# Sparse attention followed by a bilinear FFN: even and odd rows of a half dealt to two matmul positions, padded activation sums, one store per half, and one-bank PSUM tiles in the last tile's second pass

## The chip, the cores and the metric

The kernel runs on one core of a Trainium2 chip. Times are device microseconds (us) of that core for one whole launch. The core has five instruction queues that run beside each other[...]: TensorE (PE, with its weight loads shown apart as PEld), VectorE (DVE), ScalarE (ACT), GpSimd (POOL) and SyncE (SP, which only issues transfers). A line number such as L650 is a line of the kernel before the change, unless it is said to be of the changed kernel.

## The reference

Two stages are computed, the second on the output of the first. The shapes are batch 8, heads 8, sequence 576, head width 64; so 4608 tokens of width 512 enter the FFN, whose inner width is 1536.

```python
scores = scale * np.matmul(q, k.transpose(0, 1, 3, 2))
mask_local = (rel >= 0) & (rel < stride)                          # heads 0 to 3, stride 32
mask_strided = (rel >= 0) & (pos[None, :] % stride == pos[:, None] % stride)   # heads 4 to 7
...
attn = np.exp(scores - max); attn = attn / (sum + 1e-09)
x = (attn @ v).transpose(0, 2, 1, 3).reshape(4608, 512)
out = ((x @ w_a) * (x @ w_b)) @ w_out
```

## The kernel before

The work is cut twice. Attention goes batch by batch (b from 0 to 7) and each batch into eight units (S: scores, exponential and mask; V: product with v and division). The FFN goes by nine tiles of 512 tokens (t from 0 to 8). Tile t is 16 slots: slots 0 to 11 (`ffn_ab`, L548) make the inner activations of one block of 128 inner columns each. Two groups of matmuls of L545 give x·w_a and x·w_b in PSUM, ACT copies the first (L562), and DVE multiplies the two into the bf16 tile `pf` (L565). Slots 12 to 15 multiply `pf` by w_out. While the FFN of tile t runs, the attention of a later batch is put in between its matmuls, at places that the tables STEPS and LATER (L513 to L519) give, so that PE does not stand still for ACT and DVE. Tiles 7 and 8 have no attention left beside them.

Tiles 3 to 8 (FAST_Y) do the last product by a seven-product scheme for two by two blocks (Winograd's form of Strassen's scheme) in place of eight products. The tokens of a tile are split in two halves i, the output columns in two halves j, the inner dimension in even and odd blocks e. L565 writes `pf` so that the half i takes 256 columns in a row. DVE then forms five sums or differences of the quarters of `pf` (`fast_s`, L572 to L583) in the tile `ps`, numbered n = 0 to 4: L578 makes sum 0, L580 sums 1 and 2, L582 differences 3 and 4. They are made in parts, for ranges of the six pairs of inner blocks g, at the places that L868 gives: slot 4 (sum 0, g 0-1), 6 (3 and 4, g 0-1), 8 (1 and 2, g 0-1), 10 (3 and 4, g 2-3), 11 (sum 0, g 2-5; then 3 and 4, g 4-5), and 12 (1 and 2, g 2-5).

`y_plan` (L610) then runs the products in the order 3, 4, 1, 7, 5, 2, 6. Each is two positions q of six matmuls g (L650): 128 rows from `pf` or `ps` as the stationary operand, 256 columns from w_out or from a sum of its blocks as the moving operand. Products 3 and 4 read `pf`; product 1 reads sum 0, product 7 difference 4, product 5 sum 1, product 2 sum 2 and product 6 difference 3. Their results are put together by DVE (L626, L629, L631, L639), ACT (L622, L633, L635) and POOL (L636, L640), and `store_half` (L615) sends each half of the rows out on SP's queue by two transfers, one for each q.

The order of the instructions on every engine is the order in which the code issues them (`manual_schedule`, L742). Semaphore waits are put in by the framework, which compares the parts of a tile that two instructions read or write. [...]

The last tile, t = 8, uses `y_tail` (L656): first all seven products for position q = 0 (the first pass), then for q = 1 (the second pass), so that the first pass's rows leave early. The second pass has four accumulators, a, b, c and d. Before the change, a and b are the two banks of one PSUM tile (`o`), c and d the two banks of another (`st`). The order of the products is 3 (a), 4 (b), 1 (c), 2 (b), 5 (a), 6 (c), 7 (d); 3 and 4 are read by L683 and L685, 1 by L689, 2 by L693, 5 by L698, 6 by L703 and 7 by L706.

Of the kernel before, what the change touches and what calls it, by code (L numbers as in the profile page):

```python
# [7 lines left out]
F32 = mybir.dt.float32  # L8
BF16 = mybir.dt.bfloat16
I16 = mybir.dt.int16  # L10
ALU = mybir.AluOpType
# [19 lines left out]
def kernel(  # L31
# [10 lines left out]
    nc = tc.nc  # L42
# [7 lines left out]
    FD = d_ff // 128  # L50
    TTOK = 512
# [6 lines left out]
    nat = ctx.enter_context(tc.tile_pool(name="nat", bufs=1))  # L58
    sb = ctx.enter_context(tc.tile_pool(name="sb", bufs=3))
    fsb = ctx.enter_context(tc.tile_pool(name="ffn", bufs=2))  # L60
    pst = ctx.enter_context(tc.tile_pool(name="pst", bufs=1, space=bass.MemoryType.PSUM))
    dram = ctx.enter_context(tc.tile_pool(name="dram", bufs=2, space=bass.MemoryType.DRAM))

    psum4 = {}
# [98 lines left out]

    FG = FD // 2
    HT = TTOK // 2
    HN = d_model // 2
    wf = wp.tile([128, 5, FG, HN], BF16, name="wf")
    wov = wo_sb.rearrange("p (g e) (j n) -> p e j g n", e=2, j=2)
# [14 lines left out]
    shared = {}  # L183

    def load_qk(b, strided, heads=range(HL), names="kq"):
        for nm in names:
            src = {"k": k, "q": q}[nm]
            if b < FIRST_D:
                n, R, h0 = (NP, RS, HL) if strided else (96, RL, 0)
                w0 = {"k6": 0, "q6": 1536, "k8": 3072, "q8": 5120}[f"{nm}{R}"]  # L190
                if b not in shared:
                    shared[b] = nat.tile([128, 5 * FD * TTOK // 4], BF16, tag="shared", name="shared")
                t = nats[b, nm, strided] = shared[b][:n, w0:w0 + HL * R * D].rearrange("p (h r d) -> p h r d", r=R, d=D)
                hs = slice(heads[0], heads[-1] + 1)
                nc.gpsimd.dma_start(out=t[:, hs], in_=src[b, h0:h0 + HL].rearrange("h (p r) d -> p h r d", r=R)[:, hs])  # L195
            elif strided:

                t = nat_s[nm]
                n = 32 if b == FIRST_D else YS
                for h in heads:  # L200
                    nc.gpsimd.dma_start(
                        out=t[32 * h:32 * h + n],
                        in_=bass.AP(tensor=src.tensor, offset=(b * H + HL + h) * S * D,
                                    ap=[[RS * D, n], [YS * RS * D, 3], [1, RS * D]]))
            else:
                if 0 in heads:
                    nats[b, nm, strided] = nat.tile([128, NY, D], BF16, tag=f"{nm}l", name=f"{nm}l")
                t = nats[b, nm, strided]
                for h in heads:
                    nc.gpsimd.dma_start(out=t[32 * h:32 * h + 32],  # L210
                                        in_=src[b, h].rearrange("(i y) d -> y i d", y=32))
            nats[b, nm, strided] = t
# [127 lines left out]
    ps = {}  # L340
# [190 lines left out]
    def mm_bank(shape):  # L531
        nm = "tp" if used[0] % 4 == 3 and used[0] >= 0 else "mm"
        used[0] += 1
        return psum4[nm].tile(shape, F32, tag=nm, name="mm")
# [35 lines left out]
    pss = {}  # L570

    def fast_s(t, n, gs):  # L572
        if t not in pss:
            pss[t] = nat.tile([128, 5 * FD * TTOK // 4], BF16, tag="shared", name="ps").rearrange("p (g m) -> p g m", g=FG)
        s = pss[t][:, gs]
        x = pfs[t].rearrange("p (g e) (i m) -> p g e i m", e=2, i=2)[:, gs]
        if n == 0:
            nc.vector.tensor_tensor(s[:, :, 0:HT], x[:, :, 0, 0], x[:, :, 1, 1], op=ALU.add)  # L578
        elif n == 1:
            nc.vector.tensor_tensor(s[:, :, HT:3 * HT].rearrange("p g (i m) -> p g i m", i=2), x[:, :, 0], x[:, :, 1], op=ALU.add)  # L580
        else:
            nc.vector.tensor_tensor(s[:, :, 3 * HT:].rearrange("p g (e m) -> p g e m", e=2), x[:, :, :, 1], x[:, :, :, 0],  # L582
                                    op=ALU.subtract)  # L583

    yst = {}

    def products(t):
        pf, s = pfs[t], pss[t]
        full = lambda e, i: (lambda g, q: pf[:, 2 * g + e, HT * i + 128 * q:HT * i + 128 * (q + 1)])
        summed = lambda n: (lambda g, q: s[:, g, HT * n + 128 * q:HT * n + 128 * (q + 1)])  # L590
        wsum = lambda n: (lambda g: wf[:, n, g])
        wfull = lambda e, j: (lambda g: wov[:, e, j, g])
        return {"3": ("a", full(0, 0), wsum(0)), "4": ("b", full(1, 1), wsum(1)), "1": ("c", summed(0), wsum(2)),
                "2": ("b", summed(2), wfull(0, 0)), "5": ("a", summed(1), wfull(1, 1)), "6": ("c", summed(3), wsum(3)),
                "7": ("d", summed(4), wsum(4))}

    def f32t(nm):
        return fsb.tile([128, 2, HN], F32, tag=nm, name=nm, bufs=1)

    def col(j):  # L600
        return slice(HN * j, HN * (j + 1))

    def y_store(eng, t, y, i, q, n=slice(0, d_model)):
        rows = out[TTOK * t:TTOK * (t + 1), n].rearrange("(q a i s) c -> a s i q c", q=2, i=2, s=16)
        eng.dma_start(out=rows[:, :, i, q], in_=y[i][:, q, n])

    def y_bufs():
        return [fsb.tile([128, 2, d_model], F32, tag="y_sb", name="y_sb", bufs=2) for _ in range(2)]

    def y_plan(t):  # L610

        plan, bank, v = products(t), {}, {}
        y = []

        def store_half(i):  # L615
            for q in range(2):
                y_store(nc.sync, t, y, i, q)

        def post(k):
            if k == "3":  # L620
                v["a"] = v["w"] = f32t("ya")
                nc.scalar.copy(v["a"], bank["a"])  # L622
                y.extend(y_bufs())
                v["y"] = y
            elif k == "4":
                nc.vector.tensor_tensor(v["w"], bank["b"], v["a"], op=ALU.add)  # L626
            elif k == "1":
                v["e"] = f32t("ye")
                nc.vector.tensor_tensor(v["e"], bank["c"], v["w"], op=ALU.add)  # L629
            elif k == "7":  # L630
                nc.vector.tensor_tensor(v["e"], v["e"], bank["d"], op=ALU.subtract)  # L631
            elif k == "2":
                nc.scalar.copy(y[1][:, :, col(0)], bank["b"])  # L633
            elif k == "5":
                nc.scalar.copy(y[0][:, :, col(1)], bank["a"])  # L635
                do(16 * t + 15, nc.gpsimd.tensor_tensor, y[0][:, :, col(0)], v["e"], y[0][:, :, col(1)], ALU.subtract)  # L636
                do(16 * t + 18, store_half, 0)
            else:
                nc.vector.tensor_tensor(v["w"], bank["c"], v["w"], op=ALU.add)  # L639
                do(16 * t + 17, nc.gpsimd.tensor_tensor, y[1][:, :, col(1)], v["w"], y[1][:, :, col(0)], ALU.subtract)  # L640
                do(16 * t + 19, store_half, 1)

        for k in "3417526":
            b, lhs, rhs = plan[k]
            new = b not in bank
            if new:
                bank[b] = mm_bank([128, 2, HN])
            for q in range(2):
                for g in range(FG):
                    nc.tensor.matmul(bank[b][:, q], lhsT=lhs(g, q), rhs=rhs(g), start=new and q == 0 and g == 0,  # L650
                                     stop=g == FG - 1, skip_group_check=True)
                    if g == FG - 1 and q == 1:
                        post(k)
                    yield v

    def y_tail(t):  # L656

        plan, y = products(t), y_bufs()
        w, e = f32t("ya"), f32t("ye")
        v = {"a": w, "y": y}  # L660
        for q in range(2):
            if q == 0:
                bank = {x: mm_bank([128, HN]) for x in "abcd"}
            else:
                o = psum4["o"].tile([128, 2, 512], F32, tag="o", name="end")
                st = pst.tile([128, 2, 512], F32, tag="st", name="end")
                bank = {"a": o[:, 0, :HN], "b": o[:, 1, :HN], "c": st[:, 0, :HN], "d": st[:, 1, :HN]}
            c21, c12, c22 = y[1][:, q, col(0)], y[0][:, q, col(1)], y[1][:, q, col(1)]
            wq, eq = w[:, q], e[:, q]
            seen = set()  # L670
            for k in "3412567":
                b, lhs, rhs = plan[k]
# [69 lines left out]
    with tc.manual_schedule(engines={ENG.PE, ENG.SP, ENG.Pool, ENG.DVE, ENG.Activation}):  # L742
# [10 lines left out]
        for x, src in ((raw[0], k), (raw[1], q)):  # L753
            nc.sync.dma_start(out=x[:96].rearrange("p (h r d) -> p h r d", h=2, d=D),
                              in_=src[0, 0:2].rearrange("h (p r) d -> p h r d", r=RL))
# [67 lines left out]
        def do(i, fn, *args):  # L823
            at.setdefault(i, []).append(lambda: fn(*args))
# [7 lines left out]
        for b in range(FIRST_D, B):  # L832
# [7 lines left out]
            else:  # L840
# [5 lines left out]
            gs = {2: (13, 13, 14, 14, 15, 16, 17, 17, 18, 18), 3: (8, 9, 10, 11, 12, 13, 14, 15, 16, 17)}.get(b) or (  # L846
                3, 5, 7, 9, 12, 13, 14, 15, 16, 17)
# [64 lines left out]
```

The softmax here doesn't subtract the row's maximum and nothing guards it: scores larger than these inputs give would overflow.

## Time and profile before

| what | value |
|---|---|
| median of three runs | 337.68 us (337.02 to 338.57) |
| the profiled execution's own time | 336.98 us |
| its span, first to last instruction | 335.3 us |
| PE busy | 326.2 us, 97% of the span, 2814 matmuls |
| DVE busy | 254.7 us, 76% |
| ACT busy | 202.8 us, 60% |
| POOL busy | 173.4 us, 52% |
| granted TensorE clock | 0.998 of full |

The profile comes from one execution. Its span leaves out some 1.7 us that the device counts around it. A group of instructions in the profile has a line, an engine, the tiles written and read, a count and a mean duration. A matmul's duration in it (273 ns for 256 columns) [...]overlaps with the next one's; how fast matmuls follow each other is read from the chain of work that ended last or from the timeline, where 21 matmuls of 256 columns took 2.29 us, 109 ns each.

### The profile page before, as it was taken

The page shows a single profiled execution, that of the slowest core. Times are in us where ns is not written, and L with a number is a line of the kernel's source. Part 1 is how long each engine was busy: PE and PEld are TensorE (multiplying, and loading weights), DVE is VectorE, ACT ScalarE, POOL GpSimd, SP SyncE. Part 2 cuts the span into 40 slices and gives each one's busy share as a digit, 9 for nine tenths or more (in the row PEclk, how much of TensorE's full clock was granted, in tenths as well). Part 3 has the DMA queues.
Part 4 walks back from the last instruction along what each step waited for, and adds up shares of the span by engine and source line. Part 5 has one row for each costly group of instructions (what it writes and reads, how often), then busy time and mean ns, then how long its engine had stood idle before and what let it go on. Part 6 is the DMA issues. An engine that isn't in the chain of part 4 may idle for free.

```text
span 335.3 us, 7662 instructions
## 1 busy us (share of the span) xinstructions
PE 326.2 (97%) x2814; PEld 201.8 (60%) x2814; DVE 254.7 (76%) x489; ACT 202.8 (60%) x329; POOL 173.4 (52%) x295
## 2 busy tenths in 40 slices
PE   8999999999999999999999999999999999999992
PEld 6654555455555555556999885568556844674472
DVE  5867566768878985799999999999877845738641
ACT  5663955468678865776587757875788533223320
POOL 8945836499956644765577457754312031312011
PEclk9999999999999999999999999999999999999999
DMA  9999999599999599969888998899123021003013
GB/s 155 148 203 196 201 181 188 120 191 70 131 221 155 86 99 158 129 116 92 69 83 139 179 98 75 142 164 107 25 62 119 2 73 54 1 12 116 0 29 98
DMA packets 102173, 37.60 MB, mean 112 GB/s; under 512 B 77432, under 2 KB 97784, under 8 KB 102136
## 3 DMA queue, kind: packets, MB, share of 16 engines
q0 software_dynamic: 87760, 19.58, 64.4%
q1 hardware_dynamic: 14104, 17.34, 17.7%
q8 instruction: 22, 0.36, 0.4%
q10 hardware_dynamic: 272, 0.20, 0.2%
q14 instruction: 15, 0.12, 0.1%
HBM read 39.71 MB, written 9.44 MB: 147 GB/s over the span
## 4 chain that ended last, share of the span: by engine, by line
PE 75%; DMA 12%; POOL 7%; DVE 2%; issue 2%; ACT 0%; DVEq 0%; POOLq 0%
PE mm L545 44%; PE mm L650 14%; PE mm L730 7%; DMA vl<-in_v_dram 4%; PE o L454 4%; PE st L356 3%; DMA shared<-in_k_dram 3%; DMA wa_sb<-in_moe_w_a_dram 3%; PE end L678 1%; PE mm L678 1%; POOL shared L195 1%; DMA kl<-in_k_dram 1%; POOL ql L210 1%; DMA natk<-in_k_dram 1%; POOL vl L222 1%
## 5 line engine op out<-in xcount | busy, mean ns | idle before, releaser
L545 PE MATMUL mm<-xT,wb_sb 128*128 128x512 bf16 (+1 forms) x472 | 110.2, 357 | 0.1
L545 PE MATMUL mm<-xT,wa_sb 128*128 128x512 bf16 (+1 forms) x472 | 110.3, 358 | 0.0
L562 ACT COPY a_sb<-mm 128x512 f32<-128x512 f32 x106 | 62.2, 587 | 48.7 <-PE mm L545 46.4
L545 PEld LDWEIGHTS <-wb_sb 128*128 128x128 bf16 x480 | 46.4, 98 | 44.5 <-issue 0.6
L880 POOL CAST pace<-pf 1x1 f32<-1x1 bf16 x84 | 28.4, 339 | 85.1 <-DVE pf L565 73.8
L565 DVE TENSOR_TENSOR pf<-a_sb,mm 128x512 bf16<-128x512 f32 x72 | 48.5, 674 | 17.2 <-PE mm L545 13.8
L545 PEld LDWEIGHTS <-wa_sb 128*128 128x128 bf16 x480 | 42.6, 98 | 31.2
L364 ACT ACTIVATE p<-st 128x576 bf16<-128x576 f32 (+1 forms) x64 | 41.7, 651 | 9.5 <-PE st L356 9.0
L463 ACT ACTIVATE xr<-o 64x576 f32<-64x576 f32 x48 | 31.1, 648 | 26.1 <-PE o L454 25.9
L730 PE MATMUL mm<-wo_sb,pf 128*128 128x512 bf16 x144 | 34.4, 379 | 0.5 <-DMA wo_sb<-in_moe_w_out_dram 0.5
L464 ACT ACTIVATE xr<-xr 64x576 f32<-64x576 f32 x48 | 32.9, 685 | 1.5
L650 PEld LDWEIGHTS <-ps 128*128 128x128 bf16 x300 | 28.5, 98 | 4.4 <-DVE ps L578 1.2
L567 DVE TENSOR_TENSOR pf<-a_sb,mm 128x512 bf16<-128x512 f32 x34 | 23.0, 678 | 8.4 <-ACT a_sb L562 5.9
L470 DVE TENSOR_TENSOR xT<-o,xr 64x288 bf16<-64x288 f32 x48 | 21.5, 448 | 10.4 <-ACT xr L464 9.7
L468 DVE TENSOR_TENSOR xT<-o,xr 64x288 bf16<-64x288 f32 x48 | 21.5, 447 | 8.9 <-ACT xr L464 8.3
L374 DVE TENSOR_TENSOR p<-p,mask_l 128x576 int16<-128x576 int16 x32 | 19.8, 618 | 6.8 <-ACT p L364 6.7
L650 PE MATMUL mm<-wf,ps 128*128 128x256 bf16 x180 | 22.7, 273 | 0.1
L234 POOL DMA_DIRECT2D vs<-in_v_dram x24 | 19.7, 821 | 4.1 <-PE st L356 2.8
L730 PEld LDWEIGHTS <-pf 128*128 128x128 bf16 x144 | 12.9, 98 | 13.9 <-issue 0.8
L880 POOL COPY pace<-y_sb 1x1 f32<-1x1 f32 x18 | 3.2, 177 | 34.0 <-ACT y_sb L633 14.8
L210 POOL DMA_DIRECT2D ql<-in_q_dram x24 | 16.0, 666 | 6.2 <-DMA wo_sb<-in_moe_w_out_dram 4.2
L210 POOL DMA_DIRECT2D kl<-in_k_dram x24 | 16.1, 671 | 4.0 <-issue 3.8
(155 smaller groups left out, 493.7 us busy)
## 6 DMA issues: line engine op xcount, KB each, us to landing
out_dram<-y_sb SPq DMA_DIRECT2D x34, 256.0 KB
vl<-in_v_dram POOLq DMA_DIRECT2D x7, 384.0 KB, 7.2
kl<-in_k_dram POOLq DMA_DIRECT2D x24, 72.0 KB, 3.1
ql<-in_q_dram POOLq DMA_DIRECT2D x24, 72.0 KB, 3.2
vs<-in_v_dram POOLq DMA_DIRECT2D x24, 72.0 KB, 3.8
wo_sb<-in_moe_w_out_dram POOLq DMA_DIRECT2D x4, 384.0 KB, 11.2
natk<-in_k_dram POOLq DMA_DIRECT2D x20, 72.0 KB, 3.2
natq<-in_q_dram POOLq DMA_DIRECT2D x20, 72.0 KB, 3.5
```

What stands on the lines that cost most here:

```text
L210: nc.gpsimd.dma_start(out=t[32 * h:32 * h + 32], in_=src[b, h].rearrange("(i y) d -> y i d", y=32))
L364: nc.scalar.activation(p[:M, :, :W], st[:M, :, :W], ACT.Exp, scale=scale)
L463: nc.scalar.activation(r, sums, ACT.Ln)
L464: nc.scalar.activation(r, r, ACT.Exp, scale=-1.0)
L468: nc.vector.tensor_mul(dst[:, W * half:W * (half + 1)], o[:64, j, :W], r[:, j])
L545: nc.tensor.matmul(ps_[:, c0:c0 + n], lhsT=w[:, kk, 128 * f:128 * (f + 1)], rhs=xT[:, kk, x0:x0 + n], start=(kk == first and c0 == 0), sto ...
L562: nc.scalar.copy(a_sb, ab[0])
L565: nc.vector.tensor_mul(pf[:, f, :].rearrange("p (i a s) -> p a i s", i=2, s=16), halves(a_sb), halves(ab[1]))
L567: nc.vector.tensor_mul(pf[:, f, :], a_sb, ab[1])
L650: nc.tensor.matmul(bank[b][:, q], lhsT=lhs(g, q), rhs=rhs(g), start=new and q == 0 and g == 0, stop=g == FG - 1, skip_group_check=True)
L730: nc.tensor.matmul(y, lhsT=pf[:, f, 128 * j:128 * (j + 1)], rhs=wo_sb[:, f], start=(f == 0), stop=(f == FD - 1))
L880: nc.gpsimd.tensor_copy(pace, done)
```

## The change

There are four edits.

1. Within a half of 256 columns, position q took 128 neighbouring columns; it now takes every second column, from q on (`q:HT:2`). The stationary operand of L650 and L678 is so read with a step of two elements. The output rows follow: row 32a + 16i + 2s + q of the tile, where before it was 256q + 32a + 16i + s.
2. Each of the five sums in `ps` has 272 columns of room instead of 256 (SW = HT + 16). DVE's writes of sums 1 and 2, and 3 and 4, are two rows of 256 with 16 unused between them, where they were one row of 512. The tile that shares this memory (`shared`) grows with it.
3. `store_half` sends one transfer of 128 partitions with 4 KB in a row each, in place of two with 2 KB each.
4. In the second pass of `y_tail`, a is a bank of `o`, b a bank of `st`, and c and d are banks from the rotating pool that the matmuls of L545 and the first pass use (`mm_bank`, L531).

```diff
+    SW = HT + 16
...
-                    shared[b] = nat.tile([128, 5 * FD * TTOK // 4], BF16, tag="shared", name="shared")
+                    shared[b] = nat.tile([128, FG * 5 * SW], BF16, tag="shared", name="shared")
...
     def fast_s(t, n, gs):
         if t not in pss:
-            pss[t] = nat.tile([128, 5 * FD * TTOK // 4], BF16, tag="shared", name="ps").rearrange("p (g m) -> p g m", g=FG)
-        s = pss[t][:, gs]
+            pss[t] = nat.tile([128, FG * 5 * SW], BF16, tag="shared", name="ps").rearrange("p (g n m) -> p g n m", g=FG, n=5)
+        s = pss[t][:, gs, :, :HT]
         x = pfs[t].rearrange("p (g e) (i m) -> p g e i m", e=2, i=2)[:, gs]
         if n == 0:
-            nc.vector.tensor_tensor(s[:, :, 0:HT], x[:, :, 0, 0], x[:, :, 1, 1], op=ALU.add)
+            nc.vector.tensor_tensor(s[:, :, 0], x[:, :, 0, 0], x[:, :, 1, 1], op=ALU.add)
         elif n == 1:
-            nc.vector.tensor_tensor(s[:, :, HT:3 * HT].rearrange("p g (i m) -> p g i m", i=2), x[:, :, 0], x[:, :, 1], op=ALU.add)
-        else:
-            nc.vector.tensor_tensor(s[:, :, 3 * HT:].rearrange("p g (e m) -> p g e m", e=2), x[:, :, :, 1], x[:, :, :, 0],
-                                    op=ALU.subtract)
+            nc.vector.tensor_tensor(s[:, :, 1:3], x[:, :, 0], x[:, :, 1], op=ALU.add)
+        else:
+            nc.vector.tensor_tensor(s[:, :, 3:], x[:, :, :, 1], x[:, :, :, 0], op=ALU.subtract)
...
-        full = lambda e, i: (lambda g, q: pf[:, 2 * g + e, HT * i + 128 * q:HT * i + 128 * (q + 1)])
-        summed = lambda n: (lambda g, q: s[:, g, HT * n + 128 * q:HT * n + 128 * (q + 1)])
+        full = lambda e, i: (lambda g, q: pf[:, 2 * g + e, HT * i + q:HT * (i + 1):2])
+        summed = lambda n: (lambda g, q: s[:, g, n, q:HT:2])
...
-        rows = out[TTOK * t:TTOK * (t + 1), n].rearrange("(q a i s) c -> a s i q c", q=2, i=2, s=16)
+        rows = out[TTOK * t:TTOK * (t + 1), n].rearrange("(a i s q) c -> a s i q c", i=2, s=8, q=2)
...
         def store_half(i):
-            for q in range(2):
-                y_store(nc.sync, t, y, i, q)
+            rows = out[TTOK * t:TTOK * (t + 1)].rearrange("(a i s q) c -> a s i (q c)", i=2, s=8, q=2)
+            nc.sync.dma_start(out=rows[:, :, i], in_=y[i].rearrange("p q c -> p (q c)"))
...
-                o = psum4["o"].tile([128, 2, 512], F32, tag="o", name="end")
-                st = pst.tile([128, 2, 512], F32, tag="st", name="end")
-                bank = {"a": o[:, 0, :HN], "b": o[:, 1, :HN], "c": st[:, 0, :HN], "d": st[:, 1, :HN]}
+                bank = {"a": psum4["o"].tile([128, 2, 512], F32, tag="o", name="end")[:, 0, :HN],
+                        "b": pst.tile([128, 2, 512], F32, tag="st", name="end")[:, 0, :HN],
+                        "c": mm_bank([128, HN]), "d": mm_bank([128, HN])}
```

## The prediction

> **What bounds the kernel now.** I read the page first, then the chain that ended last, then the timeline of DVE and of the weight loads around the second half of a fast tile, then the timeline of the last pass. The page:
>
> ```profile
> PE 326.2 (97%) x2814; PEld 201.8 (60%) x2814; DVE 254.7 (76%) x489; ACT 202.8 (60%) x329; POOL 173.4 (52%) x295
> ...
> PE 75%; DMA 12%; POOL 7%; DVE 2%; issue 2%; ACT 0%; DVEq 0%; POOLq 0%
> ```
>
> PE is busy 97% of the span. In order of time the chain is on PE without a break from 81.5 us to 324 us: transfers are behind it only in the first 80 us. So what PE has to wait for after 81.5 us is added to the end in full, and what spares another engine or a queue is worth nothing there. In tile 3 the chain passes product 1 (its first matmuls read sum 0):
>
> ```profile
> 157.85 0.55 PE mm L650 x5
> 158.39 0.03 issue
> 158.42 0.83 PE mm L650 x6
> ```
>
> The 0.03 is a hint that PE just met something. DVE in the same stretch (start, us, line, tile), and then the weight loads:
>
> ```profile
> 157.67 0.69 DVE L578 TENSOR_TENSOR ps<-pf 128x1024 bf16<-128x1024 bf16 x1
> 158.28 0.68 DVE L582 TENSOR_TENSOR ps<-pf 128x1024 bf16<-128x1024 bf16 x1
> 158.88 0.45 DVE L374 TENSOR_TENSOR p<-p,mask_s 72x576 int16<-72x576 int16 x1
> 159.25 0.70 DVE L304 STREAM_TRANSPOSE tk<-natk 128x512 bf16<-128x512 bf16 x1
> 159.88 1.18 DVE L580 TENSOR_TENSOR ps<-pf 128x2048 bf16<-128x2048 bf16 x1
> 160.99 0.68 DVE L626 TENSOR_TENSOR ya<-mm,ya 128x512 f32<-128x512 f32 x1
> ```
>
> ```profile
> 157.90 0.21 PEld L650 LDWEIGHTS <-ps 128*128 128x128 bf16 x2
> 158.42 0.55 PEld L650 LDWEIGHTS <-ps 128*128 128x128 bf16 x6 [0.31 <-DVE ps L578]
> ```
>
> The reader is to see that DVE works without a gap and is only just in time: L578 (sum 0, g 2-5) ends at 158.36, and 0.06 later the third weight load of product 1 goes. L580 (sums 1 and 2, g 2-5) ends only at 161.06. Today nobody waits for that: product 5, which reads sum 1, gets to its third load at about 161.3 (17 loads from 159.32 on, at 109 ns). The last pass:
>
> ```profile
> 324.78 0.82 PE L678 MATMUL end<-wf,pf 128*128 128x256 bf16 x6 [0.46 <-ACT ya L683]
> 327.46 0.81 PE L678 MATMUL end<-wo_sb,ps 128*128 128x256 bf16 x6 [0.46 <-ACT y_sb L693]
> 329.51 0.49 PE L678 MATMUL end<-wf,ps 128*128 128x128 bf16 x6 [0.58 <-DVE y_sb L703]
> 330.38 0.29 DVE L706 TENSOR_TENSOR y_sb<-ye,mm 128x128 f32<-128x128 f32 x1
> ```
>
> PE stops three times, each time for a read of the bank that shares a tile with the one it wants to write. L706 then ends at 330.67, and the last store takes the rest of the span.
>
> [...] The trace has no strided load; it has fast packed ones: 8 matmuls of L454 with a load each pass in 0.26 us, 32 ns each. [...] L582, whose inputs are already rows of 256, and L578 take 0.68 and 0.69 us for 1024 columns. [...] the granted clock is 1.00 in each stretch from 152 to 330 us that I looked at.
>
> **The change, part by part.** *Padding and the waits that come with it.* The changed program, built but not run, has the same instructions in the same order on PE, DVE, ACT and POOL; its listing with semaphores differs, ahead of the last pass, in five places, one for each of tiles 3 to 7. Before, product 1's third load (g 2) waits for L578, product 7's fifth for L582, product 5's third for L580. After, the third load still waits for L578, and the fourth load of product 1 (g 3, first position) waits for the value that L580 (g 2-5) reaches; the two later waits are gone. The value is 253 in tile 3, and 254 is L626's, which fits the DVE order above. The data don't ask for this: g 3 of sum 0 is not what L580 writes. It lies between the first and last element that L580 writes, though, and the framework seems not to tell apart the new, padded and two-row access from the strided read. What is queued behind that load on PE: the rest of product 1, the attention matmuls L454, products 7, 5, 2 and 6 and the next tile. ACT (L635, L633) and DVE (L629, L631, L639) wait for those in turn, so all move together.
>
> Its price is L580's end plus 0.06 us (as for L578), less the time at which the fourth load goes today (the third's plus 0.109):
> tile 3: 161.06 + 0.06 - 158.53 = 2.59;
> tile 4: L580 from 194.35 for 1.18, third load 192.90: 195.59 - 193.01 = 2.58;
> tile 5: 228.58 + 1.18, third load 227.12: 229.82 - 227.23 = 2.59;
> tile 6: 262.18 + 1.21, third load 261.34: 263.45 - 261.45 = 2.00;
> tile 7 (no attention on DVE): 291.14 + 1.22, first load 291.45: 292.42 - 291.78 = 0.64.
> Sum 10.40. DVE isn't held up by PE meanwhile: L582, L374, L304 and L580 need nothing that PE makes after the stall. Nor does one stall shorten the next: just before each tile's end DVE waits for ACT, and so for PE, again (0.16 us at 187.18, 0.78 at 259.65), so it brings no backlog and no lead over. I see no cover for the 10.40, since PE is the chain.
>
> *Strided weights.* 504 loads of tiles 3 to 8 (six tiles, 84 each). Matmuls of 256 columns follow each other at 109 ns, a packed load needs at most 32. A load at half the rate (64) is still hidden; at a quarter (128) it costs 504 x 19 ns = 9.6 us. A gain is excluded, as the matmul's 109 ns is the limit. I take 0.
>
> *DVE's sums.* Same elements, step 1: 0. Bound above: from 1024 to 2048 columns L580 goes from 0.68 to 1.19, so 0.50 ns a column; at half the rate L582 would be 0.51 longer and L580 1.03, and each stall 1.5 longer: 7.7 us for five.
>
> *One store per half.* Ten issues fewer on SP's queue, 0.59 us each; behind them stand the copies of k and q (L314, L318). PE waits for none of these after 81.5 us, and the y buffers are used again a tile (34 us) later: 0. If that cover were gone it would be a gain of up to 0.6 an issue.
>
> *Last pass in one-bank tiles.* Group starts before: 323.50 (3), 324.78 (4), 325.43 (1), 326.18 (2), 327.46 (5), 328.11 (6), 329.51 and 329.84 (7 in two cuts). Six matmuls take 0.655. Without the three waits: 323.50, 324.16, 324.81, then product 2 still waits for L685 to read b (group 4 ends 324.98, + 0.10 + 0.42 + 0.06 = 325.56), 326.21, 326.87, 327.52, 327.85: PE gains 1.99. Next late is POOL: L694 starts when L693 ends plus 0.08 (326.86) and takes 0.73, L699 takes another 0.73 behind it and ends about 328.35; L706 follows in two parts, to 328.98 instead of 330.67. Gain 1.69. SP issues its last three stores at 326.8, 328.2 and 329.0, over 0.6 apart, so the store behind moves along. Bounds 0.5 and 2.0; I take 1.7. The new c and d banks are free by then (L698 of the first pass ends 322.76).
>
> Sum: 10.4 - 1.7 = +8.7 us. On the profiled execution, 335.3 span and 336.98 in all, this gives 344.0 and 345.7; the three runs shown have the median 337.68, 0.7 above that execution, so 346.4.
>
> **The rivals.** *Faster: the new wait is empty.* If L580's last part were done within 0.34 us of the fourth load, five stalls would stay under 1.7 and the last pass would decide: 337.7 - 1.7 = 336.0. For it: the three stops in the last pass are real, and nothing else is added to PE. Against: DVE would have to end L580 at 158.9 in tile 3 and ends it at 161.06, with L582, L374 and L304 ahead of it in a fixed order. 6%.
> *Strided weights slower than matmuls.* At a quarter of the rate 346.4 + 9.6 = 356.0. For: no strided load is in the trace. [...] 10%.
> [...] 346.4 + 7.7 = 354.1, a little more where DVE is already late for L578. Against: L582's inputs. 6%.
> *The clock falls in the stalls.* [...] 353.2. 6%.
>
> **How the numbers follow.** The forecast, 346.4, has 72%, with its own range from 345.0 to 348.0. To leave out at most 2 in 10 the range takes in the clock's rival at 353: 344.5 to 353.0. A measurement of this kernel can tell some 0.5% (1.7 us) from no change. Faster by more: 0.05; within: 0.03; slower by more: 0.92.
>
> **What would show it.** In the changed profile: a wait of the weight load of L650 on DVE's L581 (L580 of before), five times, 2.0 to 2.6 us four times and about 0.6 once; matmuls of L650 still 109 ns apart and loads still near 98 ns long; L581 and L583 as long as before; no wait of the second pass on L683, L693 or L703, and the end of L706 some 1.7 us nearer to the start of that pass. I am wrong if L650's matmuls are further apart, or if PE passes product 1 without a stop.

## The result, and the profile after

The changed kernel takes 349.38 us (median of six runs, 345.95 to 350.65); the kernel before took 337.27 us (median of six on the same footing). The ratio is 1.0344, with a 95% interval from 1.0288 to 1.0401: 12 us slower. The forecast was 346.4 us, slower, with a range from 344.5 to 353.0. The medians here and below are over all runs of a kernel, while the ratios leave out its slow runs, those over 1.5% above its fastest, such as the kernel before's 341.4 us at a mean granted clock of 0.980 beside 337.3 us at 0.997.

The profiled execution of the changed kernel took 347.10 us, its span is 345.1 us, 9.8 more than before. The page, first the busy time of each engine and then the chain that ended last by engine:

```profile
PE 327.0 (95%) x2814; PEld 202.1 (59%) x2814; DVE 255.4 (74%) x489; ACT 202.5 (59%) x329; POOL 173.2 (50%) x295
...
PE 66%; DMA 12%; POOL 10%; DVE 7%; issue 3%; ACT 2%; POOLq 0%; DVEq 0%
```

PE is no busier than before (327.0 against 326.2 us), so nothing was added to its work. DVE has 7% of the chain where it had 2%: PE now waits for it. The list of what the weight loads wait for has a new line (us in total, times, longest), beside one that was there before; the last line shown is its counterpart in the kernel before:

```profile
PEld L650 <- DVE ps L581: 10.4, 5, 2.6
...
PEld L650 <- DVE ps L579: 1.2, 4, 0.3
```

```profile
PEld L650 <- DVE ps L578: 1.2, 4, 0.3
```

Lines of the changed kernel are one higher here than before up to L583: L579, L581 and L583 are L578, L580 and L582 of before. The chain of work in tile 3, in order of time and without the pieces under 0.2 us, runs over DVE and back to PE; and the weight loads of that stretch show where PE stands:

```profile
158.85 0.69 DVE ps L579
159.54 0.26 DVE ps L583
160.14 0.29 issue
160.43 0.70 DVE tk L305
161.13 1.12 DVE ps L581
162.29 0.72 PE mm L650 x5
```

```profile
159.08 0.21 PEld L650 LDWEIGHTS <-ps 128*128 128x128 bf16 x2
159.59 0.10 PEld L650 LDWEIGHTS <-ps 128*128 128x128 bf16 x1 [0.31 <-DVE ps L579]
162.29 0.44 PEld L650 LDWEIGHTS <-ps 128*128 128x128 bf16 x5 [2.60 <-DVE ps L581]
```

Before, six loads followed each other after sum 0. Now one goes, and the next comes 2.70 us later, when sums 1 and 2 are done. What stands behind that load in PE's order stands still with it: PE is idle for 2.41 us, and the attention matmuls of L455, next after product 1, start at 162.85. The DVE operations themselves are as long as before (means of L583 for 1024 columns and L581 for 2048):

```profile
L583 DVE TENSOR_TENSOR ps<-pf 128x1024 bf16<-128x1024 bf16 x15 | 10.2, 681 | 0.0
L581 DVE TENSOR_TENSOR ps<-pf 128x2048 bf16<-128x2048 bf16 x5 | 6.0, 1194 | 0.0
```

The granted clock is worth a look by stretches. These are the stretches just behind the stalls of tiles 3, 4, 5 and 6: length, busy time and instructions of PE, PEld, DVE, ACT and POOL, and the clock as the third number from the end:

```profile
162.29:166.00 3.71, 3.71 (x40) 3.35 (x41) 1.80 (x4) 1.33 (x2) 0.00 (x0) 1.00 0.67 55
...
199.35:203.00 3.65, 3.65 (x39) 3.31 (x40) 1.74 (x4) 1.33 (x2) 0.00 (x0) 1.00 0.67 63
...
236.10:239.60 3.50, 3.44 (x23) 2.62 (x24) 0.89 (x3) 1.33 (x2) 0.00 (x0) 0.52 0.77 66
...
273.97:277.00 3.03, 3.03 (x34) 2.74 (x35) 1.15 (x3) 1.33 (x2) 0.00 (x0) 1.00 0.00 0
```

Behind tile 5's stall the clock was 0.52 for 3.5 us, and 23 matmuls fitted where the other stretches, at 1.00, held 34 to 40 in 3.0 to 3.7 us. By that clock I estimate a cost of 0.48 x 3.5 = 1.7 us. Last, the last tile, first pass and second pass: the start of the first pass before the change, then PE and the final DVE instruction of the changed kernel:

```profile
318.83 1.47 PE L678 MATMUL mm<-wf,pf 128*128 128x256 bf16 x12
```

```profile
331.88 1.47 PE L678 MATMUL mm<-wf,pf 128*128 128x256 bf16 x12
...
336.56 1.47 PE L678 MATMUL end<-wf,pf 128*128 128x256 bf16 x12
337.87 0.82 PE L678 MATMUL mm<-wf,ps 128*128 128x256 bf16 x6
338.62 1.47 PE L678 MATMUL end<-wo_sb,ps 128*128 128x256 bf16 x12
339.92 1.49 PE L678 MATMUL mm<-wf,ps 128*128 128x256 bf16 x18
...
341.37 0.48 DVE L706 TENSOR_TENSOR y_sb<-ye,mm 128x128 f32<-128x128 f32 x2
```

The three stops are gone. From the first matmul of the first pass (331.88; before, 318.83) to the end of L706 it is 9.97 us; it was 11.84. And from there to the end of the span it is 3.25 us where it was 4.63.

The account of the 9.8 us of this execution: stalls +10.4, one stretch of low clock +1.7, last pass -1.9, the end behind it -1.4, together +8.8. The missing 1.0 lies ahead of tile 3, where the chain still hangs on transfers (L579 starts at 158.85, L578 of before at 157.67): at 92.62 PE has waited 1.16 us for L471, behind a transfer of v that ended at 90.98. e1_sums_outer, below, with the same transfers, shows only 0.3 of it (its third load goes at 158.73, that of before at 158.42), so I put it down to this execution and not to the change.

### The profile page after: what moved, and what is told of

Same layout as the page of the kernel before. It is cut to its first block, busy times and chain, and to the rows that moved or that the text cites. A ratio compares the mean times of both kernels' runs of the same rounds, so it can differ in the third digit from the quotient of the medians.

```text
span 345.1 us, 7644 instructions
## 1 busy us (share of the span) xinstructions
PE 327.0 (95%) x2814; PEld 202.1 (59%) x2814; DVE 255.4 (74%) x489; ACT 202.5 (59%) x329; POOL 173.2 (50%) x295
## 4 chain that ended last, share of the span: by engine, by line
PE 66%; DMA 12%; POOL 10%; DVE 7%; issue 3%; ACT 2%; POOLq 0%; DVEq 0%
PE mm L546 43%; PE mm L650 10%; PE mm L730 5%; DMA vl<-in_v_dram 4%; PE o L455 3%; DMA shared<-in_k_dram 3%; DMA wa_sb<-in_moe_w_a_dram 3%; PE st L357 3%; DVE ps L581 2%; PE mm L678 2%; DVE xT L471 1%; POOL shared L196 1%; DMA vs<-in_v_dram 1%; DVE tk L305 1%; DVE ps L579 1%
## 5 line engine op out<-in xcount | busy, mean ns | idle before, releaser
L365 ACT ACTIVATE p<-st 128x576 bf16<-128x576 f32 (+1 forms) x64 | 41.6, 650 | 10.4 <-PE st L357 9.8
L650 PEld LDWEIGHTS <-ps 128*128 128x128 bf16 x300 | 29.1, 100 | 15.3 <-DVE ps L581 10.4
L471 DVE TENSOR_TENSOR xT<-o,xr 64x288 bf16<-64x288 f32 x48 | 21.5, 449 | 21.4 <-ACT xr L465 20.7
L650 PE MATMUL mm<-wf,ps 128*128 128x256 bf16 x180 | 24.9, 284 | 9.5 <-DVE ps L581 9.4
```

Of the source, the lines that this page charges most:

```text
L365: nc.scalar.activation(p[:M, :, :W], st[:M, :, :W], ACT.Exp, scale=scale)
L471: nc.vector.tensor_mul(dst.rearrange("d (p r) -> d p r", r=RS)[:, :, G * half:G * (half + 1)], o[:64, j, :W].rearrange("d (g p) -> d p g", ...
```

## The experiments

My theory was that a wait that the data don't ask for costs the time. The rivals were the strided weights, the padded rows on DVE, the single store, and the clock. Each run below was timed beside the kernel before on the same chip, and ratios are to that; e1, e2, e9 and e10 have 22 runs each, e3 has 9, the others 6. The first four ran together, with the kernel before at 337.04 us; the next four with it at 337.54; the last three with it at 337.31.

**e1_sums_outer: all of the change, without the wait.**

```diff
-            pss[t] = nat.tile([128, FG * 5 * SW], BF16, tag="shared", name="ps").rearrange("p (g n m) -> p g n m", g=FG, n=5)
+            pss[t] = nat.tile([128, FG * 5 * SW], BF16, tag="shared", name="ps").rearrange("p (n g m) -> p g n m", g=FG, n=5)
```

> The changed kernel with one edit: the tile of the sums is laid out with the sum's number outermost (n, g, m instead of g, n, m). Strided weights, padding, one store per half and the new last pass all stay. In the built program product 1's fourth load no longer waits for the sums 1 and 2 of g 2-5. Theory (the wait is what costs): the 10.4 us of stalls and the clock lost in them go, the gain of the last pass stays, so 334 to 336 us, a little under the kernel before (337.3). Rival, strided weights cost: stays at 345 or more. Rival, padded rows cost DVE: stays at 343 or more, since the rows are as long and as far apart within a sum as in the changed kernel.

Measured: 335.03 us, ratio 0.9927 (0.9909 to 0.9945). With the sum's number outermost, sum 0 of all g lies ahead of the first element that L581 writes. The weight loads of tile 3 again pass after sum 0:

```profile
158.22 0.21 PEld L650 LDWEIGHTS <-ps 128*128 128x128 bf16 x2
158.73 0.55 PEld L650 LDWEIGHTS <-ps 128*128 128x128 bf16 x6 [0.30 <-DVE ps L579]
```

One line of layout turns 12 us slower into 2 us faster. Strided weights, padding and the single store are all still there, so none of them costs anything that shows. The new layout has one small wait of its own, 0.5 us in the last tile, where the loads of product 2 wait for L581.

**e2_packed_reads: edits 1 and 3 undone.**

```diff
-        full = lambda e, i: (lambda g, q: pf[:, 2 * g + e, HT * i + q:HT * (i + 1):2])
-        summed = lambda n: (lambda g, q: s[:, g, n, q:HT:2])
+        full = lambda e, i: (lambda g, q: pf[:, 2 * g + e, HT * i + 128 * q:HT * i + 128 * (q + 1)])
+        summed = lambda n: (lambda g, q: s[:, g, n, 128 * q:128 * (q + 1)])
...
-        rows = out[TTOK * t:TTOK * (t + 1), n].rearrange("(a i s q) c -> a s i q c", i=2, s=8, q=2)
+        rows = out[TTOK * t:TTOK * (t + 1), n].rearrange("(q a i s) c -> a s i q c", q=2, i=2, s=16)
```

(and `store_half` with two stores again)

> The changed kernel with the positions q as 128 neighbouring columns again and with two stores per half, so edits 1 and 3 undone; padding and the new last pass stay. The built program has the waits of the kernel before. Theory (the strided read, not the padding, makes the framework put in the wait): 334 to 336 us. If padding were to blame for the time: 345 or more.

Measured: 336.25 us, ratio 0.9971 (0.9954 to 0.9989), 0.25 above the expected span. The padding is in, the wait is not: its list of waits has no line of L650 behind L581. The 1.2 us to e1_sums_outer were not explained by my theory; e9 and e10 take them up.

**e3_last_pass_alone: the kernel before with edit 4 only.**

```diff
-                o = psum4["o"].tile([128, 2, 512], F32, tag="o", name="end")
-                st = pst.tile([128, 2, 512], F32, tag="st", name="end")
-                bank = {"a": o[:, 0, :HN], "b": o[:, 1, :HN], "c": st[:, 0, :HN], "d": st[:, 1, :HN]}
+                bank = {"a": psum4["o"].tile([128, 2, 512], F32, tag="o", name="end")[:, 0, :HN],
+                        "b": pst.tile([128, 2, 512], F32, tag="st", name="end")[:, 0, :HN],
+                        "c": mm_bank([128, HN]), "d": mm_bank([128, HN])}
```

> The kernel before with only the last pass's one-bank tiles. Predicted gain 1.7 us to the last DVE instruction; the changed kernel's profile shows 1.9 there and another 1.4 from that instruction to the end. Theory: 334 to 336 us. Rival, that the rest after the last instruction is chance: 335.5 to 336.

Measured: 335.82 us, ratio 0.9956 (0.9937 to 0.9974): 0.0044 x 337 = 1.5 us of gain. The theory's span holds it, and the rival's, 335.5 to 336, too. In its profile the stretch from the first matmul of the first pass (319.42) to the end of the last DVE instruction (329.37) is 9.95 us, as in the changed kernel, and the span ends at 334.5, 5.1 us later. So the last pass gives its gain, but the shorter end of the changed kernel does not come from it.

**e4_strided_unpadded: the kernel before with edits 1 and 3.**

```diff
-        summed = lambda n: (lambda g, q: s[:, g, HT * n + 128 * q:HT * n + 128 * (q + 1)])
+        summed = lambda n: (lambda g, q: s[:, g, HT * n + q:HT * (n + 1):2])
```

(and the same for `full`, the rows and `store_half` as in the change)

> The kernel before with strided reads, rows dealt by even and odd position, and one store per half; no padding and the old last pass. The built program has the wait of product 1's fourth load all the same. Theory: before (337.3) + 10.4 of stalls + 1.7 to 7 of lost clock, so 349 to 354 us. If padding made the wait or the time: 337 us.

Measured: 348.76 us, ratio 1.0347 (1.0311 to 1.0384), 0.2 below the expected span. Its list of waits has the same five (L580 is L581 of the changed kernel):

```profile
PEld L650 <- DVE ps L580: 10.4, 5, 2.6
```

The strided read, on the unpadded tile, makes the wait and the time; that edit 3, which came along, does neither is seen in e1, where it stays and costs nothing. This settles what my prediction left vague: padding and two-row writes have no part in it.

**e5_fill: the idle time filled with matmuls.**

```diff
                 bank[b] = mm_bank([128, 2, HN])
+                if k == "1" and 3 <= t <= 6:
+                    for x in range(22 if t < 6 else 17):
+                        nc.tensor.matmul(bank[b][:, 0], lhsT=plan["3"][1](x % FG, 0), rhs=plan["3"][2](x % FG),
+                                         start=True, stop=True, skip_group_check=True)
```

> The changed kernel with idle time filled: ahead of product 1 of tiles 3 to 6, 22, 22, 22 and 17 more matmuls of 256 columns are put, written to the bank that product 1 then overwrites (their results are not used). At 109 ns each they take 2.4 us and 1.9 us, about as long as the stall, so the weight load that waits for sums 1 and 2 hardly waits any more, and PE is never idle for long. Theory (10.4 us of waiting, and on top the clock that falls in the idle time): same waiting in effect, no lost clock, granted clock 0.995 or more, so 344 to 346 us, 3 to 5 less than the changed kernel although PE does 9 us more work. Rival, the spread of the changed kernel between 346 and 351 us comes from elsewhere (transfers at the start): 347 to 351.

Measured: 344.77 us, ratio 1.022 (1.0191 to 1.025). The weight loads of its tile 3, where the 22 of L650 are the filling (the loads of the products are L654 in this kernel):

```profile
157.22 2.39 PEld L650 LDWEIGHTS <-pf 128*128 128x128 bf16 x22
159.62 0.32 PEld L654 LDWEIGHTS <-ps 128*128 128x128 bf16 x3
160.43 0.44 PEld L654 LDWEIGHTS <-ps 128*128 128x128 bf16 x5 [0.49 <-DVE ps L581]
```

PE does 83 x 0.109 = 9.0 us more work, and the kernel is 4.1 us faster than the changed kernel run beside it (e8, 348.84; by the ratios 3.4, and their intervals do not meet). All six runs of e5_fill were granted a mean clock of 0.999 or 1.000. So the wait itself is worth 344.77 - 335.03 = 9.7 us on top of e1_sums_outer (measured on another chip), and the idle time in it some 4 more.

**e6_sums_12_first: a shorter wait.**

```diff
-                                    (12, 1, 2, 6)):
+                                    (11, 1, 2, 6)):
```

> The changed kernel with the last part of sums 1 and 2 (g 2-5) issued at the end of slot 11 instead of slot 12, so that on DVE it stands ahead of the mask L374 and the transpose L304 rather than behind them (names of the kernel before). Its end comes 1.0 us earlier after sum 0 in tiles 3 to 5 and 0.4 in tile 6. Theory: stalls of 1.6, 1.6, 1.6, 1.6 and 0.6, in sum about 7.0 instead of 10.4, and less lost clock: 341 to 344 us. Rival, the time does not hang on this wait: 347 to 351.

Measured: 340.65 us, ratio 1.0113 (1.0081 to 1.0144), 0.3 below the expected span. The list of waits:

```profile
PEld L650 <- DVE ps L581: 7.2, 5, 1.6
```

7.2 us of stalls where 7.0 were expected, and no lost clock that shows: the six runs were granted 0.995 to 1.000. In time: 335.03 + 7.2 = 342.2 expected from e1_sums_outer, 340.65 measured on another chip; the 1.5 between them is not explained.

**e7_two_stores: e1_sums_outer with two stores per half.**

```diff
-            rows = out[TTOK * t:TTOK * (t + 1)].rearrange("(a i s q) c -> a s i (q c)", i=2, s=8, q=2)
-            nc.sync.dma_start(out=rows[:, :, i], in_=y[i].rearrange("p q c -> p (q c)"))
+            for q in range(2):
+                y_store(nc.sync, t, y, i, q)
```

> As e1_sums_outer (335.0 us), but with two stores per half again, the strided rows kept. Prediction's value for the single store is 0: 335.0. If the single store is what makes e1_sums_outer 1.2 us faster than e2_packed_reads: 336.2.

Measured: 335.20 us, ratio 0.9933 (0.9907 to 0.9958), no difference from e1_sums_outer. The single store is worth nothing that can be measured here.

**e8_after_again: the changed kernel as the yardstick.**

> The changed kernel once more on the same chip, as the yardstick for the runs above and to see several profiles' clocks. Theory: 346 to 350 us, longer where the granted clock is lower, by some 1.7 us for each 0.005 of the mean clock.

Measured: 348.84 us, ratio 1.032 (1.028 to 1.036). Over both measurements of the changed kernel, the three runs with a mean clock of 0.995 took 345.9, 346.0 and 347.1 us, the one with 0.990 took 347.9, the six with 0.984 or 0.985 took 348.8 to 349.9, and the two with 0.980 took 350.7 and 351.7. From the first to the third group the mean clock falls by 0.011, and 0.011 x 347 = 3.8 us of clock lost; 3.0 us lie between their means. Its profiled execution has the same 10.4 us of stalls and, behind tile 5's, the same fall.

**e9_rows_in_8: e1_sums_outer with the rows in 8 blocks.**

```diff
-            halves = lambda x: x.rearrange("p (a i s) -> p a i s", i=2, s=16)
-            nc.vector.tensor_mul(pf[:, f, :].rearrange("p (i a s) -> p a i s", i=2, s=16), halves(a_sb), halves(ab[1]))
+            halves = lambda x: x.rearrange("p (a i s) -> p a i s", i=2, s=32)
+            nc.vector.tensor_mul(pf[:, f, :].rearrange("p (i a s) -> p a i s", i=2, s=32), halves(a_sb), halves(ab[1]))
...
-        rows = out[TTOK * t:TTOK * (t + 1), n].rearrange("(a i s q) c -> a s i q c", i=2, s=8, q=2)
+        rows = out[TTOK * t:TTOK * (t + 1), n].rearrange("(a i s q) c -> a s i q c", i=2, s=16, q=2)
```

> As e1_sums_outer (335.0 us: strided reads, even and odd rows, one store), but the rows of a half are dealt in blocks of 32 instead of 16, so that a store's rows in memory are 8 blocks of 16 pairs and not 16 blocks of 8. Nothing else changes. Seen so far: from the last DVE instruction to the end the profiles with 16 blocks take 3.0 to 4.0 us, those with 8 blocks (before, the packed reads, the last pass alone) 4.6 to 5.4. Theory of the blocks: [...] the end takes 4.6 to 5.4 again and the time is 336.2 to 337. Theory of the strided rows or of chance: 335.0.

Measured: 336.49 us, ratio 0.997 (0.9952 to 0.9989), against 0.9927 (0.9909 to 0.9945) of e1_sums_outer; the intervals do not meet (two chips, each ratio to the kernel before on its own). The end takes 4.5 us in its profile (329.63 to 334.1), 0.1 below the expected span.

**e10_last_and_16: the last pass and 16 blocks, all else as before.**

```diff
-            halves = lambda x: x.rearrange("p (a i s) -> p a i s", i=2, s=16)
+            halves = lambda x: x.rearrange("p (a i s) -> p a i s", i=2, s=8)
...
-        rows = out[TTOK * t:TTOK * (t + 1), n].rearrange("(q a i s) c -> a s i q c", q=2, i=2, s=16)
+        rows = out[TTOK * t:TTOK * (t + 1), n].rearrange("(q a i s) c -> a s i q c", q=2, i=2, s=8)
```

(on top of e3's edit; the write of `pf` goes with `halves`)

> The kernel before with the new last pass (e3_last_pass_alone, 335.8 us) and the rows of a half dealt in blocks of 8 instead of 16, so that each store's rows are 16 blocks of 8 neighbouring rows. Reads stay packed, two stores per half, no padding. Theory of the blocks: the end takes 3.0 to 4.0 us, 334.3 to 335.0 us, as fast as e1_sums_outer without its strided reads, padding or single store. Otherwise: 335.8. If DVE pays for writing pf in rows of 8: more.

Measured: 335.28 us, ratio 0.9934 (0.9913 to 0.9955), as fast as e1_sums_outer within the intervals; 0.3 us above the expected span, and the end in its profile, 4.1 us, is a little longer than expected too. Its interval overlaps e3's, from which it differs by 0.7 us in ratio, so this run alone would not show that the blocks matter; e9 does, with one edit.

**e11_sum_0_first: and sum 0 ahead of the attention's division.**

```diff
-            for slot, n, z0, z1 in ((4, 0, 0, 2), (6, 2, 0, 2), (8, 1, 0, 2), (10, 2, 2, 4), (11, 0, 2, 6), (11, 2, 4, 6),
+            for slot, n, z0, z1 in ((4, 0, 0, 2), (6, 2, 0, 2), (8, 1, 0, 2), (10, 2, 2, 4), (10.75, 0, 2, 6), (11, 2, 4, 6),
...
+            for f in at.get(i - 0.25, ()):
+                f()
             take(i)
```

> As e10_last_and_16, and sum 0's last part (g 2-5) stands on DVE straight behind the last product of pf in slot 11, ahead of the attention's division (L470 of the kernel before). This takes away the wait that the kernel before has too: product 1's third weight load behind L578, about 0.2 us of PE in each of tiles 3 to 6. Theory: 0.8 us less than e10_last_and_16, about 334. If the division, now 0.7 us later, holds up the next tile: the same or more.

Measured: 334.51 us, ratio 0.9897 (0.9861 to 0.9934). This is the lowest median of all versions, 0.8 below e10 as expected, though its interval overlaps those of e1 and e10, so the gain is not shown by time. In its list of waits the line of L650 behind L578 is gone.

## Why the prediction was right, and where not

**The wait.** Right in place, number and size. Five stalls were forecast with a sum of 10.40; the profile has five with 10.4, the longest 2.6. e1 takes the wait away and with it the loss; e6 shortens it and the loss shrinks with it. What failed is the half sentence on its cause: "the framework seems not to tell apart the new, padded and two-row access from the strided read". e4 and e2 show that the strided read is enough and that padding is innocent. What was not tried is which rule of the framework's comparison does it; that a layout with sum 0 outside the written span cures it (e1) fits a comparison of first and last elements. So does the short wait in e1's last tile: in its layout L581 (sums 1 and 2 of g 5 there) writes from sum 1 to sum 2, and what lies between, sum 2 of g 0 to 4, waits too.

**The clock.** This is the term that was mis-sized. The prediction put it at 0 and, as a rival with 6%, at 6.8 us (353.2), an estimate that rested on no trace. The runs: some 4 us, in the middle (348.84 against 344.77 with the idle time filled). That the stops cause it is shown by how often the clock is low: a mean of 0.990 or less was granted in 9 of 12 runs of the changed kernel, in none of the six of e5 and none of the six of e6, and in 9 of the 100 runs of the kernel before that stand beside the experiments. So a low mean clock is not by itself the mark of a stop. How many stops are hit in one run is an estimate: a stretch of 3.5 us at 0.52 takes 0.48 x 3.5 / 345 = 0.005 off the mean, which makes one hit at 0.995 and four at 0.980. Two of the changed kernel's runs at 0.995 have a trace, with one such stretch each; none of its runs with a lower mean has one.

In the profiled execution PE stood still for 2.4 us in tile 5's stall (of the 5.10 us before 236.10, 2.72 busy), and the clock was 0.52 for the 3.5 us behind it. Tile 3's stop was as long (4.29 us before 162.29, 1.85 busy), and the clock behind it was 1.00 for 3.71 us; which stop is hit, and why, stays open. With stalls of at most 1.6 us (e6) the six runs were granted 0.995 to 1.000.

**The last pass.** Forecast 1.69 to the last DVE instruction; 1.87 in the profile, and 1.5 in time for it alone (e3). POOL as the next late engine was right: in the changed kernel L699 runs from 340.60 to 341.33 and L706 starts at 341.37.

**What the sum left out.** "I take 1.7", with the store behind moving along, missed that edit 1 also changes the stores of the last tile: their rows come in 16 blocks instead of 8, and the end shrinks from 4.63 to 3.25 us. Why 16 blocks end sooner is not shown: the trace does not show the transfer engines one by one. Below is the mean busy share of the 16 engines, in tenths for each 0.7 us from 318 us on: the kernel before and e9, both with 8 blocks, stay at 5 or less, and e1, with 16, reaches 9.

```profile
DMA  0000000001445543335452000000000000000000
```

```profile
DMA  0000000000054455545530000000000000000000
```

```profile
DMA  0000000000399106677000000000000000000000
```

The highest rate in one of these slices is 202, 197 and 366 GB/s. That the blocks are what counts in time is shown by e9 against e1 (1.5 us). What stays open: among the profiles with 16 blocks the end is 3.3 us with one store per half (the changed kernel, e1, e8) and 4.0 to 4.1 with two (e7, e10, e11), though the times of e1 and e7 do not differ.

**The zeros.** Strided weights: right. In the changed kernel's last 18 matmuls, 6 of 256 columns take 0.655 and the run's overlap 0.165, which leaves (1.49 - 0.82) / 12 = 56 ns for each of 128 columns, as with packed weights before (0.33 us for six). DVE: right, 681 and 1194 ns against 680 and 1193. The store: right (e7).

So the point, 346.4, was 3 us low because two terms were missing that partly cancel: +4 to 5 for the clock, -1.4 for the blocks. The measured 349.38 lies above the forecast's own 345.0 to 348.0, and inside the whole range only because that was drawn up to the clock's rival at 353. That the profiled execution, at 347.10, comes so near the point is luck: in it one hit of the clock, +1.7, and the shorter end, -1.4, all but cancel.

## What to carry to other kernels

After an access is made strided, list the waits of the built program again: a read that steps through a tile can be taken to meet a neighbouring write that it only interleaves with (here five waits, 10.4 us), and the remedy here was a layout in which the written span and the read span are apart. Here a stop of TensorE cost its own length and, where PE stood still for 2.4 us, at times some 1.7 us more, a stretch of 3.5 us at a clock of 0.52; filling it with idle matmuls showed which part is which. When rows of an output are dealt anew, look at the outermost count of the store at the very end of the kernel: 16 blocks in place of 8 were worth 1.5 us here (e1 against e9).

## What the runs showed that I had not expected

Nine us of useless matmuls made a kernel 4 us faster (e5): they stood in time that was idle anyway, and with them the granted clock was 0.999 or 1.000 in all six runs. And the kernel's gain, where the wait is gone, is some 2.2 to 2.5 us (e10, e1) from two small places at its very end, one of which was not an aim of any edit.
